# Moving one group of w_in weight sums on VectorE, in a fused linear attention and MLP kernel

## The chip, the cores and the metric

The kernel runs on one core of one Trainium2 chip. The metric is the device time of one execution in microseconds (us), as the median of several runs; lower is better. The engines are named as in the profile: PE is TensorE (matrix products), with PEld for its weight loads, DVE is VectorE, ACT is ScalarE, POOL is GpSimd, and SP is SyncE, which here issues most of the DMAs.

## The reference

The first part is linear attention with a decay per head, worked through in blocks with a running state; the second is a two-layer MLP over its output.

```python
# q, k, v: (4, 8, 768, 64) float32, lam: (8,)
for b in range(nb):                       # blocks of 64 positions
    intra = (qb @ kb^T * Dmask) @ vb      # inside the block, decay lam ** (i - j) for i >= j
    inter = (qb * lam_pow) @ kv_state     # from the state before the block
    out[:, :, sl] = intra + inter
    kv_state = lam_block * kv_state + (kb * rev_pow)^T @ vb
x = out.transpose(0, 2, 1, 3).reshape(3072, 512)
h = x @ w_in                              # (512, 2048)
g = h * sigmoid(1.702 * h)
return g @ w_out                          # (2048, 512)
```

## The kernel before, in words

The 3072 tokens are worked in six waves (0 to 5) of 512 tokens each. A wave goes through the attention part, which leaves its transposed result in `xT`, through the first product with `w_in` and the activation on ACT, which leaves `g_sb`, and through the second product with `w_out`, which goes out to `out`. The waves overlap: while the MLP of wave w runs, the attention of wave w + 1 is made between its steps. Waves 0 and 1 use one layout of the attention (functions with the prefix `d_`, two halves each, called by `start` and `end`), waves 2 to 5 another (prefix `n_`, whose state is carried on from wave to wave).

Both products of the MLP are done, for most of their blocks, in a Strassen-like form with seven products in place of eight. This needs sums and differences of the operands: of the tokens (`x_sums`, line 529, tiles `x_s`; `g_sums`, line 441, tiles `g_s`, whose parts the text calls s1 to s4), and of the weights (`in_sums`, line 520, tiles `w_in_t`; `weight_sums`, line 428, tiles `w_out_t`). All of these are made by DVE. The weight sums are made once and kept. `in_sums(g)` handles group g of the first product's blocks; there are four groups. Groups 0, 1 and 3 are summed in wave 0. Group 2 takes its four blocks from one tile of `w_in`, so its sums are four instructions over 128 x 512 elements, in bf16. Wave 1 uses the sums of groups 0 and 3 alone; waves 2 to 5 use those of all four groups.

The order of the work is written out by hand, with the scheduler set to manual, so each engine's queue has its instructions in the order in which the program calls them. Waves 1 to 5 have a list of steps each in `STEPS`, and `one_step` turns a name into calls. The names that matter here:

- `I2` is `in_sums(2)`.
- `S0` to `S3` are the next wave's scores on PE (line 335). `M0`, `M2` are masks made by DVE alone (line 348), `m1`, `m3` masks scaled by ACT (line 344) and multiplied by DVE (line 345).
- `gl1`, `gl2`, `gh12`, `gl4`, `gh4` are instructions of `g_sums` on DVE.
- `P` with two digits is a product of the second layer on PE (line 461): the first digit is the number of the product, the second the token half. Products 1, 6, 5 and 3 accumulate one behind the other in one PSUM bank, `ps_X`, and what lies in it is read out between them (lines 474 and 485, into `part` and `o_sb`).
- `R` is the rest of the next wave's attention: PE's products (lines 377, 390) and the state products (line 364), which DVE adds to the state in four instructions (line 368).
- `+a1`, `+a2` are the first products of the next wave's first layer (line 544), `X` its `x_sums`, `G` a small copy on POOL that makes it wait for `x_s`. Behind it POOL scales the q and k of the wave after (line 209), and SP transposes them by DMA (line 245).

The steps of wave 1 follow a stretch that isn't in `STEPS`: the end of wave 0's MLP, mixed with the attention of wave 1. There `start(1, 1)` makes scores on PE and masks on DVE (line 267), and `end(1, 0)` and `end(1, 1)` finish with a state update on DVE (line 716).

Of the kernel before, what the change touches and what calls it, by code (L numbers as in the profile page):

```python
# [25 lines left out]
def kernel(  # L26
# [205 lines left out]
    def turn_pe(w, c, nm, copy=act_copy, g=None):  # L232
        x = cast[w, c, nm]
        rr = list(range(NP)) if g is None else [2 * g, 2 * g + 1]
        t = acc("ps_t", bf16, [P, len(rr), 2, P])
        for i, r in enumerate(rr):
            for a in range(2):
                nc.tensor.transpose(t[:, i, a, :], x[:, a, r * P : (r + 1) * P], ident)
        if g in (None, 0):
            trans[w, c, nm] = work.tile([P, 2 * NP, P], bf16, tag=f"{nm}T{c}", bufs={"k": 1, "q": 2}[nm], name=f"{nm}T")  # L240
        copy(trans[w, c, nm][:, 2 * rr[0] : 2 * rr[0] + 2 * len(rr)], t.rearrange("p r a s -> p (r a) s"))
# [323 lines left out]
    def one_step(w, s):  # L565
# [45 lines left out]
        else:  # L611
            raise ValueError(s)

    STEPS = {
# [24 lines left out]
    with tc.manual_schedule():  # L639
# [63 lines left out]
        def end(w, c):  # L703
            oa, oz = d_out(w, c)
            t = acc("ps_kv", shape=[P, NP, D]) if w else states[w, c]
            if w == 0:
                nc.scalar.copy(seen, oz[:, 3, P - 1 : P])
            d_state(w, c, t, Z)
            if w == 0:
                d_inter(w, c, oz, 0, False)  # L710
            if w and c == 0:
                d_one(w, 1)
            d_x(w, c, 0, oa, act_copy)
            d_x(w, c, 1, oz, act_copy if w and c else dve_copy)
            if w:
                nc.vector.tensor_tensor(kv_sb[0][:, 2 * w + c], kept[w, c], t, op=ADD)
            else:
                nc.scalar.copy(kv_sb[0][:, 2 * w + c], t)
            if w and c == 0:
                d_keep(w, 1)  # L720

        def steps(w, names):
            for s in names.split():
                one_step(w, s)
# [21 lines left out]
        steps(0, "P51")  # L746
        turn_pe(1, 1, "k", act_copy)
        end(1, 0)
        steps(0, "P30")
        turn_pe(1, 1, "q", act_copy)  # L750
        halves = [(c, fc) for c in range(HF) for fc in HALVES]
        for i, (c, fc) in enumerate(halves):
# [47 lines left out]
```

## Time and profile before

| | |
|---|---|
| median of 3 runs | 193.56 us (193.47 to 193.85) |
| the profiled execution | 193.77 us, span 192.1 us |
| granted TensorE clock, mean | 1.00 |
| line 520, all 20 instructions on DVE | 20.4 us to 68.5 us after the span's start; the 12 of 128 x 512 take 0.42 us each |

The span runs from the first to the last instruction of the profiled execution; the rest of its time lies around it. The profile gives the start and length of each instruction, the idle time of an engine just before it, and what released it (written `<-`). A line such as `sm<-ps_s` names the tile that is written and the one that is read; `x4` is the count of instructions that are merged into one row. A matmul's end is modelled, so where PE is followed step by step the starts are the better measure.

### The profile page before, as it was taken

Reading aid. Unit: us, or ns where it says so; the run is one execution under the profiler, and the core shown is the slowest. Engines: PE = TensorE matmul, PEld = TensorE weight load, DVE = VectorE, ACT = ScalarE, POOL = GpSimd, SP = SyncE. Lnnn points to the kernel's source line nnn. Section 1 sums busy time; section 2 is a strip of 40 time slices with the busy share of each in tenths; the row PEclk is TensorE's granted clock in tenths of the full one; section 3 lists DMA queues with packets and bytes.
Section 4 is the critical chain, followed back from the end, with each engine's and each line's share of the span. In section 5 each row is a group of like instructions: output and inputs, shape, how many; then the busy total and the mean of one; then the engine's idle time right before and its main releaser. Section 6 shows DMA issues by size and latency. Waiting matters only on the chain.

```text
span 192.1 us, 5543 instructions
## 1 busy us (share of the span) xinstructions
PE 185.1 (96%) x2295; PEld 152.6 (79%) x2297; DVE 153.7 (80%) x292; ACT 129.7 (68%) x242; POOL 53.1 (28%) x76
## 2 busy tenths in 40 slices
PE   7988999999999999999999999999999999999993
PEld 2556645888888887888888888888888888888882
DVE  1777689798477799979799879799889797889950
ACT  4956676257776985379896388895388875597711
POOL 5597000048467000096000295000393000000000
DMA  5999999988997799988998746999365903300113
GB/s 148 322 277 206 206 206 216 275 251 235 238 226 169 172 253 208 221 190 130 209 227 193 237 129 147 216 245 257 109 165 117 212 3 112 110 3 0 52 58 112
DMA packets 89599, 33.91 MB, mean 177 GB/s; under 512 B 67430, under 2 KB 89446, under 8 KB 89574
## 3 DMA queue, kind: packets, MB, share of 16 engines
q1 hardware_dynamic: 84676, 28.84, 60.3%
q0 software_dynamic: 4896, 4.72, 14.3%
q8 instruction: 18, 0.29, 0.7%
q14 instruction: 7, 0.06, 0.1%
q10 hardware_dynamic: 2, 0.00, 0.0%
HBM read 27.26 MB, written 6.29 MB: 175 GB/s over the span
## 4 chain that ended last, share of the span: by engine, by line
PE 80%; DVE 9%; DMA 4%; SPq 3%; issue 1%; ACT 1%; ACTq 0%
PE ps_X L461 20%; PE ps_hX L544 16%; PE ps_V L461 9%; PE ps_hV L544 8%; PE ps_h L402 5%; PE ps_h L414 5%; PE ps_Q L461 5%; PE ps_hQ L544 4%; DMA qf<-in_q_dram 4%; SPq L84 3%; DVE sm L267 2%; DVE g_s L441 2%; PE ps_s L335 2%; PE ps_o L390 2%; DVE sm L348 1%
## 5 line engine op out<-in xcount | busy, mean ns | idle before, releaser
L461 PEld LDWEIGHTS <-g_s 128*128 128x128 bf16 x384 | 36.9, 98 | 5.7 <-DVE g_s L441 0.4
L563 ACT ACTIVATE g_sb<-h_sb 128x512 bf16<-128x512 f32 x54 | 32.6, 631 | 1.2 <-DVE h_sb L552 1.2
L544 PEld LDWEIGHTS <-w_in_t 128*128 128x128 bf16 x288 | 28.2, 98 | 3.3
L461 PEld LDWEIGHTS <-g_sb 128*128 128x128 bf16 x288 | 27.4, 98 | 4.1
L221 ACT COPY part<-ps_hX 128x512 f32<-128x512 f32 x32 | 18.3, 586 | 11.5 <-PE ps_hX L544 11.5
L461 PE MATMUL ps_X<-w_out_t,g_s 128*128 128x256 bf16 x192 | 23.3, 273 | 0.2 <-DVE g_s L441 0.2
L544 PEld LDWEIGHTS <-w_in 128*128 128x128 bf16 x216 | 21.1, 98 | 2.4
L544 PE MATMUL ps_hX<-x_s,w_in_t 128*128 128x256 bf16 x144 | 21.6, 272 | 0.0
L441 DVE TENSOR_TENSOR g_s<-g_sb 128x1024 bf16<-128x1024 bf16 x24 | 16.3, 686 | 6.0 <-ACT g_sb L563 5.6
L209 POOL TENSOR_TENSOR qs<-qf,q_pow 128x512 bf16<-128x512 f32 x16 | 16.7, 1068 | 3.0 <-ACT xT L221 3.0
L209 POOL TENSOR_TENSOR ks<-kf,k_pow 128x512 bf16<-128x512 f32 x16 | 16.6, 1063 | 2.4 <-ACT qT L221 2.4
L634 POOL CAST behind_q<-x_s 1x1 f32<-1x1 bf16 x3 | 0.5, 174 | 59.7 <-DVE x_s L529 59.7
L474 ACT COPY part<-ps_X 128x512 f32<-128x512 f32 (+1 forms) x14 | 7.3, 523 | 13.1 <-PE ps_X L461 13.1
L218 DVE COPY part<-ps_hV 128x512 f32<-128x512 f32 x18 | 12.4, 688 | 4.3 <-PE ps_hV L544 4.3
L552 DVE TENSOR_TENSOR h_sb<-part,ps_hX 128x512 f32<-128x512 f32 x18 | 12.3, 681 | 2.7 <-PE ps_hX L544 2.7
L552 DVE TENSOR_TENSOR h_sb<-part,ps_hV 128x512 f32<-128x512 f32 x18 | 12.3, 683 | 1.0 <-PE ps_hV L544 1.0
L461 PE MATMUL ps_X<-w_out,g_sb 128*128 128x256 bf16 x96 | 12.6, 273 | 0.0
L461 PE MATMUL ps_Q<-w_out,g_sb 128*128 128x256 bf16 x96 | 12.5, 273 | 0.0
L552 DVE TENSOR_TENSOR h_sb<-part,ps_hQ 128x512 f32<-128x512 f32 x18 | 12.2, 679 | 0.0
L221 ACT CAST v_sb<-vf 128x1024 bf16<-128x1024 f32 (+1 forms) x13 | 11.3, 884 | 1.1 <-DMA vf<-in_v_dram 1.0
L461 PE MATMUL ps_V<-w_out_t,g_sb 128*128 128x256 bf16 x96 | 12.0, 273 | 0.0
L461 PE MATMUL ps_X<-w_out,g_s 128*128 128x256 bf16 x96 | 11.6, 272 | 0.2 <-DVE o_sb L485 0.2
(111 smaller groups left out, 358.8 us busy)
## 6 DMA issues: line engine op xcount, KB each, us to landing
kf<-in_k_dram SPq DMA_DIRECT2D x10, 512.0 KB, 6.9
qf<-in_q_dram SPq DMA_DIRECT2D x10, 512.0 KB, 6.7
vf<-in_v_dram SPq DMA_DIRECT2D x10, 512.0 KB, 6.0
out_dram<-o_sb SPq DMA_DIRECT2D x24, 128.0 KB, 2.4
out_dram<-o_sb SPq DMA_DIRECT2D x12, 256.0 KB, 2.9
w_out<-in_moe_w_out_dram POOLq DMA_DIRECT2D x4, 512.0 KB, 15.4
kf<-in_k_dram SPq DMA_DIRECT2D x4, 256.0 KB, 3.1
qf<-in_q_dram SPq DMA_DIRECT2D x4, 256.0 KB, 4.5
```

The lines of the kernel that those rows point to most:

```text
L84: (nc.gpsimd if w == 0 and c and nm == "v" else nc.sync).dma_start(out=x[:, h : h + n], in_=src[2 * w + c, h : h + n, 0 : 2 * P, :].rearra ...
L209: eng.tensor_tensor(x.rearrange("p b (r i j d) -> p j (b r) i d", i=2, j=2, d=D)[:, j], f.rearrange("p h (a d) -> p (h a) d", a=2).rearran ...
L218: nc.vector.tensor_copy(out, in_)
L221: nc.scalar.copy(out, in_)
L402: nc.tensor.matmul(h, w_in_sb[j][:, kc, i * P : (i + 1) * P], xT[w][:, kc, :], start=(kc == 0), stop=(kc == KC - 1))
L414: nc.tensor.matmul(h[:, u, :], w_in_sb[j][:, kc, i * P : (i + 1) * P], xT[w][:, kc, cols], start=(kc == 0), stop=(kc == KC - 1))
L441: nc.vector.tensor_tensor(o, x, y, op=f)
L461: nc.tensor.matmul(bank[:, t], x[:, m, t * P : (t + 1) * P], y, start=(n in (1, 2, 7) and t == ts[0] * last and m == 0), stop=(m == FFC // ...
L474: nc.scalar.copy(part[w, n, t.start][:, t], bank[:, t])
L544: nc.tensor.matmul(bank[:, u], z[:, kc], y[:, kc], start=(n in (1, 2, 7) and u + kc == 0), stop=(kc == 1), skip_group_check=True)
L552: nc.vector.tensor_tensor(h, h_part[w, g, {2: 1, 5: 7, 4: 6}[n]], bank, op=ADD)
L563: nc.scalar.activation(g_of[w][:, a : b + 1 : b - a, 256 * i : 256 * i + 256], bank, GELU)
```

## The change

The step `I2` is taken out of wave 1's list, where it stood between the `g_sums` of `gh3` and the scores and masks of wave 2, and put behind `P30` in the stretch before, right behind `end(1, 0)`. There the DVE instructions in front of it are those of wave 1's first state update (line 716), and the next ones behind it the masks of `start(1, 1)` (line 267). The four instructions and their operands are the same. No other engine gets or loses an instruction, and the order of the others is as before.

```diff
     STEPS = {
-        1: ("a1 a7v a2 a6 b1 b7v A2 a5 b2 b6 B2 a4 a3 b5 b4 A5 P10 A4 b3 gl3 B4 B5 P11 gh3 I2 S0 S1 M0 P20 m1 "
+        1: ("a1 a7v a2 a6 b1 b7v A2 a5 b2 b6 B2 a4 a3 b5 b4 A5 P10 A4 b3 gl3 B4 B5 P11 gh3 S0 S1 M0 P20 m1 "
             "Lk gl1 P70 P71 gl2 P21 v0 gh12 S2 S3 M2 m3 v1 o P40 P41 P60 gl4 gh4 P61 R P50 P51 +a1 X +a2 P30 "
             "P31 "),
...
         end(1, 0)
-        steps(0, "P30")
+        steps(0, "P30 I2")
         turn_pe(1, 1, "q", act_copy)
```

## The prediction

> **What bounds the kernel now.** I began with the busy shares on the page, to see which engine fills the span.
>
> ```profile
> PE 185.1 (96%) x2295; PEld 152.6 (79%) x2297; DVE 153.7 (80%) x292; ACT 129.7 (68%) x242; POOL 53.1 (28%) x76
> ```
>
> TensorE (PE) is busy for 96% of the span, VectorE (DVE) for 80%. So a saving on DVE is worth something only where PE waits for DVE. The next view is the chain of waits, in the stretch around the sums that are moved (line 520); it gives start, length, engine and line.
>
> ```profile
> 66.34 0.69 DVE g_s L441
> 67.03 0.35 DVE w_in_t L520
> 67.38 0.02 issue
> 67.40 0.49 DVE w_in_t L520 x2
> ...
> 79.09 0.61 DVE o_sb L485
> 79.70 0.04 issue
> 79.74 1.91 PE ps_X L461 x16
> ```
>
> From 66.3 to 79.7 us the chain lies on DVE, and the sums are links of it: they are not free where they are. The chain does not say how much a shorter DVE would gain, since PE may have work of its own in that time. Other waves tell that. Waves 1, 2 and 3 issue the same matmuls from the next wave's first scores (line 335, step S0) to step P30 (the last `ps_X<-w_out,g_s` group). I asked for these three stretches. The columns are the stretch, its length, the busy time of PE, PE's weight loads, DVE, ACT and POOL, then the granted clock, the DMA share and GB/s.
>
> ```profile
> 65.96:79.74 13.78, 13.37 (x217) 11.24 (x217) 13.30 (x27) 9.48 (x16) 0.00 (x0) 1.00 1.01 228
> 94.68:107.78 13.10, 13.10 (x218) 11.33 (x218) 11.96 (x23) 9.56 (x17) 0.00 (x0) 1.00 0.99 232
> 122.72:135.81 13.09, 13.09 (x217) 11.31 (x217) 11.95 (x23) 9.55 (x17) 0.00 (x0) 1.00 1.01 244
> ```
>
> The clock was 1.00 in all three and PE's work the same, yet wave 1 takes 13.78 us and the others 13.10 and 13.09. DVE carries four instructions more there (27 against 23): the sums. The excess is 13.78 - 13.10 = 0.68 us. PE's timeline shows where it lies. Wave 1:
>
> ```profile
> 65.96 0.62 PE L335 MATMUL ps_s<-qT,kT 64*128 64x128 bf16 x16
> 72.42 0.60 PE L461 MATMUL ps_X<-w_out_t,g_s 128*128 128x256 bf16 x4
> 73.19 1.48 PE L461 MATMUL ps_X<-w_out_t,g_s 128*128 128x256 bf16 x12 [0.17 <-DVE g_s L441]
> 74.61 0.64 PE L377 MATMUL ps_o<-qT,kv 64*64 64x128 bf16 x32
> 76.70 1.92 PE L461 MATMUL ps_X<-w_out_t,g_s 128*128 128x256 bf16 x16
> 78.46 0.60 PE L544 MATMUL ps_hX<-xT,w_in 128*128 128x256 bf16 x4
> 79.74 1.91 PE L461 MATMUL ps_X<-w_out,g_s 128*128 128x256 bf16 x16 [0.24 <-DVE o_sb L485]
> ```
>
> The same steps in wave 2:
>
> ```profile
> 101.15 1.91 PE L461 MATMUL ps_X<-w_out_t,g_s 128*128 128x256 bf16 x16
> 102.99 0.64 PE L377 MATMUL ps_o<-qT,kv 64*64 64x128 bf16 x32
> 105.08 1.92 PE L461 MATMUL ps_X<-w_out_t,g_s 128*128 128x256 bf16 x16
> 107.78 1.91 PE L461 MATMUL ps_X<-w_out,g_s 128*128 128x256 bf16 x16
> ```
>
> The groups at 72.42 and 101.15 are the steps P60 and P61, those at 76.70 and 105.08 P50 and P51. P60 and P61 take 74.61 - 72.42 = 2.19 us up to the next group in wave 1 and 102.99 - 101.15 = 1.84 in wave 2: in wave 1 PE stops after four matmuls for the upper half of s2 (line 441) and loses 0.35. P30 starts 79.74 - 76.70 = 3.04 after P50 in wave 1 and 107.78 - 105.08 = 2.70 after it in wave 2: it accumulates into the bank that DVE must read first for `o_sb` (line 485), and loses 0.34. Together that is 0.69, the excess of the windows but for rounding.
>
> **What leaves the old place.** DVE's rows there, and one of ACT:
>
> ```profile
> 66.95 0.42 DVE L520 TENSOR_TENSOR w_in_t<-w_in 128x512 bf16<-128x512 bf16 x1
> 68.42 1.40 DVE L348 SCALAR_TENSOR_TENSOR sm<-ps_s,inv_pow,mask 128x512 bf16<-128x512 f32 x2
> 72.45 0.69 DVE L441 TENSOR_TENSOR g_s<-g_s,g_sb 128x1024 bf16<-128x1024 bf16 x1
> 77.44 1.65 DVE L368 SCALAR_TENSOR_TENSOR kv<-kv,blk_pow,ps_kv 128x256 bf16<-128x256 bf16 x4
> 79.01 0.68 DVE L485 TENSOR_TENSOR o_sb<-part,ps_X 128x512 f32<-128x512 f32 x1
> 67.19 1.28 ACT L344 ACTIVATE sm<-ps_s,inv_pow 128x512 bf16<-128x512 f32 x2
> ```
>
> The four sums hold DVE from 66.95 to 68.42, so what is queued behind them can start up to 68.42 - 66.95 = 1.47 us earlier. I follow it step by step. PE's scores of S0 and S1 are done at 65.96 + 0.62 = 66.58, so the masks of line 348 can go at 66.95 and end at 66.95 + 1.40 = 68.35. The next masks want ACT's half of the work, which ends at 67.19 + 1.28 = 68.47: at most 0.12 is lost there. The upper half of s2 then starts at 72.45 - 1.47 = 70.98 and is ready at 71.67, or 0.12 later, before P60 begins at 72.42. The first stall goes whole, with over 0.6 us to spare.
>
> PE is then 0.35 earlier at P50: 76.70 - 0.35 = 76.35. Ahead of it stand the state products that the four updates of line 368 read. DVE could begin the updates at 77.44 - 1.47 = 75.97; waiting for PE it begins at 76.35 at the latest, as the last state product is issued by then, and they end at 76.35 + (79.01 - 77.44) = 77.92. P51 ends 78.46 - 76.70 = 1.76 after P50 begins, at 78.11. So DVE now waits for PE at `o_sb`, not PE for DVE's backlog, as in wave 2, and P30 follows P50 by wave 2's 2.70: 76.35 + 2.70 = 79.05 against 79.74, or 0.69 earlier. What is late next is that same bank, which DVE can read only when P51 is done; waves 2 and 3 have it too.
>
> **What comes into the new place.** DVE's rows there:
>
> ```profile
> 47.22 0.41 DVE L716 TENSOR_TENSOR kv<-half,ps_kv 128x256 bf16<-128x256 f32 x1
> 50.48 2.48 DVE L267 TENSOR_TENSOR sm<-ps_s,mask_d 128x512 bf16<-128x512 f32 x4 [2.85 <-PE ps_s L259]
> ```
>
> Behind the state update (line 716, done at 47.63) DVE idles 2.85 us, until PE's scores release the masks of line 267 at 50.48. At 1.47 us the four sums run from about 47.65 to 49.12 and leave 1.36. The cover is thus DVE's wait for PE. No wait is added that could last: wave 0's dense products have read the same weights by then, and nothing reads the sums before wave 2. Queued behind them on DVE are the masks, then line 716 and `x_s`, and these keep their time as long as the sums end by 50.48. The edit moves no DMA, and PE, ACT, POOL and SP hold the same instructions in the same order in both kernels' listings.
>
> The one neighbour that could lengthen the sums is POOL:
>
> ```profile
> 49.47 2.05 POOL L209 TENSOR_TENSOR ks<-kf,k_pow 128x512 bf16<-128x512 f32 x2 [2.37 <-ACT qT L221]
> 54.47 2.50 POOL L209 TENSOR_TENSOR qs<-qf,q_pow 128x512 bf16<-128x512 f32 x2 [2.95 <-ACT xT L221]
> 56.10 1.15 DVE L529 TENSOR_TENSOR x_s<-x_s,xT 128x512 bf16<-128x512 bf16 x1
> 80.39 0.43 DVE L529 TENSOR_TENSOR x_s<-x_s,xT 128x512 bf16<-128x512 bf16 x1
> ```
>
> One and the same DVE operation, of the sums' shape, took 1.15 us with POOL multiplying beside it and 0.43 with POOL idle. In the new place POOL idles from 49.47 - 2.37 = 47.10 to 49.47, waiting for ACT, so the sums end some 0.3 us before it starts. If the last one slips it costs 0.72 more and still ends about 49.9. I take 1.47 for the four, as in the old place, where POOL was idle too (0.00 in the window); the upper bound is 4 x 1.15 = 4.60. A gain in the new place itself is excluded, as DVE's next work waits for PE either way.
>
> The Trainium skill, "SBUF — State Buffer", section "Who interferes with whom", speaks against the new place, which has POOL's multiplies near: a VectorE instruction with two SBUF inputs contends with a GpSimd instruction that reads SBUF, and whichever comes second is blocked. The two `x_s` rows agree with it (1.15 against 0.43). Were POOL at work throughout, the sum by this rule would be that of the slower rival; with POOL idle it leaves the forecast as it stands.
>
> **Rivals.** Slower: the sums meet POOL's multiplies all along and take 4.60 us, from 47.65 to 52.25. The masks of line 267 start 52.25 - 50.48 = 1.77 late, and PE's products with them by about as much; less the 0.69 won later this is 1.08 slower, 194.64 us. It costs from the point where the four take over 50.48 - 47.65 = 2.83 us, nearly twice their present time, and outweighs the gain at 3.5. For it speaks how close POOL stands, against it that POOL's wait ends with ACT and not with anything moved.
>
> Half the gain: the updates of line 368 get their input later than I take it, `o_sb` with them, and only the first stall goes: 193.56 - 0.35 = 193.21. It bites once they start after 78.11 - 1.57 = 76.54, only 0.19 behind my 76.35, and takes all of the second gain 0.34 later. Against it stands wave 2, which has the same order and no such loss.
>
> Nothing gained: wave 2 can't start its scores earlier, because its transposed q comes no sooner.
>
> ```profile
> 89.59 1.24 SPq L245 DMA_TRANSPOSE qT<-qs  x1
> qT<-qs SPq DMA_TRANSPOSE x8, 2.7
> 94.68 0.62 PE L335 MATMUL ps_s<-qT,kT 64*128 64x128 bf16 x16
> 81.34 0.18 POOL L634 CAST behind_q<-x_s 1x1 f32<-1x1 bf16 x1 [19.97 <-DVE x_s L529]
> ```
>
> The last transpose is issued at 89.59 and lands 2.7 later, at 92.3, which is 2.4 us ahead of the scores at 94.68; the margin is over three times the shift. And the gate at 81.34, which POOL's casts and so the transposes follow, is released by `x_s`, so it moves along. The price would be at most the whole gain: 193.56. The same time would come out if the sums were not where the change says; the listing has them right behind line 716.
>
> **Numbers.** The profiled execution took 193.77 us at a span of 192.1; one like it would take 193.77 - 0.68 = 193.09. It lies 0.21 above the median of the three runs shown (193.56), and that difference I leave as it is: 193.56 - 0.68 = 192.88. A change of 0.2% is 0.39 us, about the least that a measurement of this kernel can tell from none. Chances: the forecast 0.82, half the gain 0.05, nothing gained 0.09 (0.02 of it for sums that are elsewhere), slower 0.04. So faster by over 0.2% has 0.82, within 0.2% 0.05 + 0.09 = 0.14, slower 0.04. The range leaves out the last two cases (0.13): its bottom is the lowest run less the forecast gain, 193.47 - 0.68 = 192.79, its top the case of half the gain, 193.21, each widened by the 0.09 between the lowest run and the median: 192.7 to 193.3.
>
> **What would show it.** Right: rows of line 520 on DVE from about 47.7, of some 0.42 each, and the idle time ahead of line 267 down from 2.85 to about 1.3; the masks of line 348 some 1.5 us earlier, directly behind `g_s`; P60 and P61 in one piece; wave 1's stretch from S0 to P30 at 13.1; later waves the same but 0.68 earlier. Wrong: sums of 1 us with POOL's line 209 beside them, masks of line 267 that start after 50.5, an idle PE ahead of wave 2's scores, or a P60 or P30 that still waits as long.

## The result and the profile after

The changed kernel took 192.63 us (median of 14 runs; 192.19 to 193.53, and one run of 195.44 at a granted clock of 0.982, which the ratio leaves out). The kernel before, run beside it and with its earlier runs, took 193.51 us (14 runs, 192.77 to 194.62). The medians lie 0.88 us apart. The ratio is 0.995, with a 95% interval of 0.9927 to 0.9973: faster by 0.97 us, or anything from 0.52 to 1.41. The profiled execution took 192.84 us at a span of 191.1.

The predicted direction is right, and the predicted 0.68 us lies within that interval. The predicted range does not hold: 192.63 is 0.07 below its bottom of 192.7.

First the stretches of the changed kernel, with the columns as before. The first row is wave 1 from S0 to P30, the second the same in wave 2.

```profile
65.72:78.81 13.09, 13.09 (x217) 11.31 (x217) 12.05 (x23) 9.08 (x16) 0.00 (x0) 1.00 0.97 223
93.74:106.85 13.11, 13.11 (x217) 11.31 (x217) 11.96 (x23) 9.56 (x17) 0.00 (x0) 1.00 1.03 246
46.37:65.72 19.35, 19.18 (x253) 16.61 (x250) 17.02 (x24) 13.96 (x27) 9.07 (x8) 1.00 0.90 209
```

Wave 1 now takes the 13.09 us of the other waves, with 23 instructions on DVE instead of 27. The third row is the part ahead of S0, from the `ps_X<-w_out,g_s` group at 46.37 on, with the new place in it. PE was not busy throughout there, 19.18 of 19.35 us. PE's timeline of the changed kernel shows both:

```profile
46.37 1.05 PE L461 MATMUL ps_X<-w_out,g_s 128*128 128x256 bf16 x8
...
52.77 0.31 PE L316 MATMUL ps_o<-sm,v_sb 64*64 64x128 bf16 x8 [0.17 <-DVE sm L267]
...
72.18 1.91 PE L461 MATMUL ps_X<-w_out_t,g_s 128*128 128x256 bf16 x16
74.02 0.64 PE L377 MATMUL ps_o<-qT,kv 64*64 64x128 bf16 x32
76.11 1.92 PE L461 MATMUL ps_X<-w_out_t,g_s 128*128 128x256 bf16 x16
...
78.81 1.91 PE L461 MATMUL ps_X<-w_out,g_s 128*128 128x256 bf16 x16
```

P60 and P61 run in one piece (74.02 - 72.18 = 1.84), and P30 follows P50 by 78.81 - 76.11 = 2.70: both stalls are gone, at the sizes read off wave 2. But at 52.77 there is a stall: PE waits for a mask of line 267. The kernel before did not have it; there the same 32 matmuls run in one piece:

```profile
52.55 0.77 PE L316 MATMUL ps_o<-sm,v_sb 64*64 64x128 bf16 x32
```

DVE's rows in the new place of the changed kernel, and then POOL's, say why.

```profile
46.74 0.41 DVE L716 TENSOR_TENSOR kv<-half,ps_kv 128x256 bf16<-128x256 f32 x1
47.07 0.42 DVE L520 TENSOR_TENSOR w_in_t<-w_in 128x512 bf16<-128x512 bf16 x1
47.52 0.42 DVE L520 TENSOR_TENSOR w_in_t<-w_in,w_in_t 128x512 bf16<-128x512 bf16 x1
47.87 1.27 DVE L520 TENSOR_TENSOR w_in_t<-w_in 128x512 bf16<-128x512 bf16 x1
49.06 1.26 DVE L520 TENSOR_TENSOR w_in_t<-w_in,w_in_t 128x512 bf16<-128x512 bf16 x1
50.25 2.47 DVE L267 TENSOR_TENSOR sm<-ps_s,mask_d 128x512 bf16<-128x512 f32 x4
```

```profile
47.78 2.27 POOL L209 TENSOR_TENSOR ks<-kf,k_pow 128x512 bf16<-128x512 f32 x2 [1.76 <-DMA kf<-in_k_dram]
```

The first two sums took 0.42 us, the other two 1.27 and 1.26. POOL began to multiply at 47.78, 0.09 ahead of the third. The sums ended at 50.3, the masks no longer waited for PE but for DVE, and the part ahead of S0 grew from 65.96 - 46.85 = 19.11 to 19.35. So the new place was not free in this execution: it cost 0.24.

The whole span, by starts on PE, then reads as follows. The head runs up to the `ps_X<-w_out,g_s` group, the second part from there to S0, the third from S0 to P30, the fourth from P30 to the end, by the span that the trace holds to 0.001 us (192.065 before, 191.141 after). POOL's start is that of its first line 209 row, counted from the end of the head.

| kernel | head | to S0 | S0 to P30 | rest | POOL's start |
|---|---|---|---|---|---|
| before | 46.85 | 19.11 | 13.78 | 112.33 | 2.62 |
| changed | 46.37 | 19.35 | 13.09 | 112.33 | 1.41 |

The span is 0.92 us shorter: 0.48 in the head, where nothing is edited, and 0.69 from S0 to P30, less 0.24 in the second part; the rest is the same to 0.01. The experiments ask which of these the change makes.

### The profile page after: what moved, and what is told of

Its sections match the earlier page's. It is cut to its first block, busy times and chain, and to the rows that moved or that the text cites. A ratio compares the mean times of both kernels' runs of the same rounds, so it can differ in the third digit from the quotient of the medians.

```text
span 191.1 us, 5544 instructions
## 1 busy us (share of the span) xinstructions
PE 184.6 (97%) x2297; PEld 152.2 (80%) x2297; DVE 156.3 (82%) x292; ACT 129.6 (68%) x242; POOL 53.7 (28%) x76
## 4 chain that ended last, share of the span: by engine, by line
PE 73%; DMA 11%; DVE 8%; POOL 2%; ACT 2%; issue 1%; SPq 0%; ACTq 0%
PE ps_X L461 19%; PE ps_hX L544 16%; PE ps_V L461 9%; PE ps_hV L544 8%; PE ps_Q L461 5%; DMA w_in<-in_moe_w_in_dram 5%; PE ps_hQ L544 4%; DVE w_in_t L520 3%; DMA kf<-in_k_dram 3%; DMA vf<-in_v_dram 3%; PE ps_h L414 2%; PE ps_s L335 2%; PE ps_o L390 2%; PE ps_fill L147 2%; POOL ks L202 1%; DVE sm L267 1%
## 5 line engine op out<-in xcount | busy, mean ns | idle before, releaser
L563 ACT ACTIVATE g_sb<-ps_hX 128x512 bf16<-128x512 f32 x18 | 10.6, 588 | 1.8 <-PE ps_hX L544 1.8
L461 PE MATMUL ps_V<-w_out_t,g_s 128*128 128x256 bf16 x96 | 11.6, 273 | 0.0
```

Of the source, the lines that this page charges most:

```text
L461: nc.tensor.matmul(bank[:, t], x[:, m, t * P : (t + 1) * P], y, start=(n in (1, 2, 7) and t == ts[0] * last and m == 0), stop=(m == FFC // ...
L563: nc.scalar.activation(g_of[w][:, a : b + 1 : b - a, 256 * i : 256 * i + 256], bank, GELU)
```

## The experiments

The first theory is that the change gives 0.69 and pays 0.24 when POOL begins before the third sum, and that the head is chance. The rivals are that the head belongs to the change, and that the 0.24 belongs to the place and not to POOL. The four parts of all profiled executions come first; each kernel is then taken up, with its edit against the changed kernel.

| kernel | head | to S0 | S0 to P30 | rest | POOL's start |
|---|---|---|---|---|---|
| changed, again | 46.41 | 19.35 | 13.09 | 112.33 | 1.31 |
| changed, POOL behind the fourth sum | 46.33 | 19.11 | 13.09 | 112.35 | 2.52 |
| sums behind the second state update | 47.17 | 21.27 | 13.10 | 112.35 | 1.74 |
| sums in wave 0 | 46.45 | 19.12 | 13.09 | 112.33 | 1.72 |
| before, again | 47.33 | 19.12 | 13.79 | 112.34 | 1.69 |
| one sum moved | 48.11 | 19.12 | 13.33 | 112.34 | 1.75 |
| two sums moved | 46.88 | 19.11 | 13.10 | 112.34 | 2.06 |
| no sums | 47.22 | 19.11 | 13.10 | 112.32 | 2.57 |
| changed, POOL behind the first sum | 45.82 | 19.11 | 13.10 | 112.34 | 1.91 |
| changed, POOL behind the second sum | 45.93 | 19.11 | 13.09 | 112.35 | 2.14 |
| changed, third profile | 47.46 | 19.12 | 13.09 | 112.35 | 2.40 |
| changed, fourth profile | 47.08 | 19.11 | 13.10 | 112.34 | 1.91 |

**The changed kernel again.** No edit.

> The changed kernel once more, unedited, for a second profile beside the kernel before. I split the execution at three starts on PE: the head, up to the `ps_X<-w_out,g_s` group in front of the new place's transposes (46.85 us before, 46.37 after); from there to S0 (19.11 before, 19.35 after); from S0 to P30 (13.78 before, 13.09 after); and the rest. Theory: the two stalls (0.69) are gone for good, the head's 0.48 is chance, since nothing is edited there, and the 0.24 that the second part lost comes from POOL's first line 209 instruction starting at 47.78 while the sums ran, so it is there again only if POOL starts before about 48.6. Expected: S0 to P30 13.1; second part 19.1 to 19.4 according to POOL's start; head anywhere from 46.3 to 47.0. Rival: the change shortens the head too (by something that I don't see); then the head is near 46.4 again and the whole is 0.9 faster. Time by the theory 0.45 to 0.7 us under the kernel before, by the rival 0.9.

192.55 us against 193.26 (33 runs), ratio 0.9948 (0.9925 to 0.997). POOL began at 1.31, and the second part was 19.35 again. The head of 46.41 and the 1.0 us that the ratio gives (0.58 to 1.45) are what the rival expected, so it stands for now.

**POOL held back.**

```diff
         steps(0, "P30 I2")
+        gate_pool(TI[2][3][0:1, 0, 0, 0:1])
```

> The changed kernel with one small POOL copy that reads the last of the four sums, put right behind them, so that POOL's multiplies (line 209) can't start while the sums run. Theory (POOL's multiplies lengthened the last two sums from 0.42 to 1.27 and 1.26 us and so held up the masks of line 267): all four sums take 0.42, the masks start with PE's scores again, the second part is 19.1 and S0 to P30 13.1; POOL's multiplies start 1 to 2 us later than they could, and nothing waits for them, since their q comes later still. Time 0.7 us under the kernel before. Rival (the sums are long for another reason, DMA traffic or the place itself): two of them still take 1.2 us and more and the second part stays at 19.35.

`gate_pool` is the small copy on POOL of one element (line 634); POOL's queue reaches its multiplies only behind it.

The rows of DVE and then of POOL in this kernel:

```profile
47.03 0.42 DVE L520 TENSOR_TENSOR w_in_t<-w_in 128x512 bf16<-128x512 bf16 x1
47.48 0.43 DVE L520 TENSOR_TENSOR w_in_t<-w_in,w_in_t 128x512 bf16<-128x512 bf16 x1
47.83 0.42 DVE L520 TENSOR_TENSOR w_in_t<-w_in 128x512 bf16<-128x512 bf16 x1
48.16 0.42 DVE L520 TENSOR_TENSOR w_in_t<-w_in,w_in_t 128x512 bf16<-128x512 bf16 x1
49.96 2.48 DVE L267 TENSOR_TENSOR sm<-ps_s,mask_d 128x512 bf16<-128x512 f32 x4 [1.38 <-PE ps_s L259]
```

```profile
48.71 0.18 POOL L634 CAST behind_q<-w_in_t 1x1 f32<-1x1 bf16 x1 [2.22 <-DVE w_in_t L520]
48.85 2.04 POOL L209 TENSOR_TENSOR ks<-kf,k_pow 128x512 bf16<-128x512 f32 x2
```

The same four instructions in the same place take 0.42 each, DVE has 1.38 us left before the masks, which wait for PE again, and the second part is 19.11. So the place is not at fault. The time was 192.51 us, ratio 0.995 (0.9925 to 0.9975); next to the changed kernel's 0.9948, the 0.24 is too small to be seen in the times.

**The sums beside POOL.**

```diff
-        steps(0, "P30 I2")
+        steps(0, "P30")
...
                 end(1, 1)
+                steps(0, "I2")
```

> The four sums behind the second state update of wave 1 (line 716, at 53.6 us) instead of the first, right ahead of `x_s`, where POOL's multiplies run from 53.0 to 59.8 us. Theory (POOL's multiplies lengthen sums): the four take 1.15 to 1.27 each, 4.6 to 5 us in all, `x_s` starts near 59 and not at 54.2, and PE waits for it ahead of the first `ps_hV<-x_s` group: the second part is 1.3 to 2.0 us longer than 19.1, S0 to P30 13.1; time 0.6 to 1.3 us over the kernel before. Rival (place and POOL don't matter, four sums are 1.47 us): `x_s` starts 1.5 us later and is ready in time, the second part stays at 19.1, time 0.7 under the kernel before.

DVE, POOL, and the two places where PE waited, in this kernel:

```profile
54.46 0.88 DVE L520 TENSOR_TENSOR w_in_t<-w_in 128x512 bf16<-128x512 bf16 x1
55.37 1.15 DVE L520 TENSOR_TENSOR w_in_t<-w_in,w_in_t 128x512 bf16<-128x512 bf16 x1
56.44 1.26 DVE L520 TENSOR_TENSOR w_in_t<-w_in 128x512 bf16<-128x512 bf16 x1
57.63 1.26 DVE L520 TENSOR_TENSOR w_in_t<-w_in,w_in_t 128x512 bf16<-128x512 bf16 x1
58.82 2.45 DVE L529 TENSOR_TENSOR x_s<-xT 128x512 bf16<-128x512 bf16 x2
```

```profile
54.01 2.23 POOL L209 TENSOR_TENSOR qs<-qf,q_pow 128x512 bf16<-128x512 f32 x2 [3.05 <-DMA qf<-in_q_dram]
56.20 2.41 POOL L209 TENSOR_TENSOR ks<-kf,k_pow 128x512 bf16<-128x512 f32 x2
58.58 2.41 POOL L209 TENSOR_TENSOR qs<-qf,q_pow 128x512 bf16<-128x512 f32 x2
```

```profile
60.14 0.60 PE L544 MATMUL ps_hV<-x_s,w_in_t 128*128 128x256 bf16 x4 [1.22 <-DVE x_s L529]
61.79 0.61 PE L544 MATMUL ps_hX<-x_s,w_in_t 128*128 128x256 bf16 x4 [0.62 <-DVE x_s L529]
```

With POOL multiplying all along, the four sums hold DVE from 54.46 to 58.82, 4.36 us where the old place took 1.47. `x_s` is late and PE stands twice; the second part is 21.27, or 2.16 longer (expected 1.3 to 2.0; the second stall had not been counted). The time was 195.25 us, ratio 1.0083 (1.0049 to 1.0117), that is 1.6 us slower, where 0.6 to 1.3 was expected; the parts give 2.16 - 0.69 = 1.47. This is the slower rival of the prediction, one state update later.

**The sums in wave 0.**

```diff
-        steps(0, "P30 I2")
+        steps(0, "P30")
...
-            steps(0, {5: "I1", 7: "I3", 9: "I0 gl3 gl1", 11: "W01234 gl2", 13: "W11234 gl4"}.get(fc, ""))
+            steps(0, {5: "I1", 7: "I2 I3", 9: "I0 gl3 gl1", 11: "W01234 gl2", 13: "W11234 gl4"}.get(fc, ""))
```

> The four sums in wave 0, ahead of group 3's sums, where DVE waited 1.2 us (before) and 1.6 us (after) for a DMA of w_in, and POOL has no arithmetic. Theory: 0.42 each, 1.5 in all, mostly inside that wait; group 3's sums and what follows may be up to 0.5 us later and DVE makes that up before PE needs its second-layer sums; so head as in the kernel before (46.3 to 47.0), second part 19.1, S0 to P30 13.1, time 0.7 us under the kernel before, the best of these four with the gated one. Rival (DVE is short of time in wave 0, too): PE waits in the head for `g_s` or `w_out_t`, head about 1 us longer, time the same as the kernel before or slower.

The parts are those of the kernel with POOL held back: 19.12 and 13.09, with a head of 46.45. 192.51 us, ratio 0.994 (0.9913 to 0.9967). The sums fit into DVE's wait for w_in, of which 1.09 us is left behind them, and POOL has no arithmetic near them.

**The kernel before as its own change.** No edit.

> The kernel before, unedited, as if it were a change. It gives a second profile of the kernel before, with its head. Theory (the head, up to the `ps_X<-w_out,g_s` group, varies by chance, as nothing ahead of it is edited in the changed kernel; it was 46.85 us before and 46.33 to 47.17 in the five edited ones): ratio 1.000 within its interval; a head anywhere from 46.3 to 47.2; second part 19.11, S0 to P30 13.78. Rival (the changes shorten the head): a head of 46.85 again, as in the first profile.

193.4 us against 193.6 (23 runs), ratio 0.9986 (0.996 to 1.0013). The second and third part repeated to 0.01 us, the head did not: 47.33 after 46.85. The two profiles of the kernel before differ in the head alone.

**One sum and two sums moved.** `in_sums` gets a list of the sums to make; in the first kernel the first is made in the new place and the other three in the old, in the second kernel two and two.

```diff
-    def in_sums(g):
+    def in_sums(g, which=(0, 1, 2, 3)):
...
-            for o, x, y in ((t1, b12, b11), (t2, b22, t1), (t3, b22, b12), (t4, b21, t2)):
+            ops = ((t1, b12, b11), (t2, b22, t1), (t3, b22, b12), (t4, b21, t2))
+            for o, x, y in [ops[n] for n in which]:
```

> Only the first of the four sums moved to the new place, the other three left ahead of wave 2's masks. It tells how the two stalls depend on DVE's backlog. By the rows of before it takes 67.40 - 66.95 = 0.45 us out of the old place: the upper half of s2 is ready at 73.14 - 0.45 = 72.69, ahead of PE's want at 72.86, so the first stall goes whole; P30 still waits for `o_sb`, which ends 0.45 earlier. Theory (P30 is set by DVE's backlog until that is gone): S0 to P30 is 13.78 - 0.45 = 13.33. Rival (the two stalls are paid off in proportion to what is moved, a quarter of 0.69): 13.61.

> The first two of the four sums moved, two left. They hold DVE from 66.95 to 67.74, 0.79 us, which is more than the 0.69 that the stalls cost. Theory: S0 to P30 is 13.09 to 13.1 already, as with all four moved, and the other two could stay for nothing; the two moved end some 0.8 us behind the state update, before POOL's line 209 begins, so the second part is 19.11. Rival (in proportion): 13.78 - 0.35 = 13.43.

PE's timeline of the kernel with one sum moved:

```profile
67.23 0.62 PE L335 MATMUL ps_s<-qT,kT 64*128 64x128 bf16 x16
73.69 1.91 PE L461 MATMUL ps_X<-w_out_t,g_s 128*128 128x256 bf16 x16
77.62 1.92 PE L461 MATMUL ps_X<-w_out_t,g_s 128*128 128x256 bf16 x16
80.56 1.91 PE L461 MATMUL ps_X<-w_out,g_s 128*128 128x256 bf16 x16
```

S0 to P30 is 80.56 - 67.23 = 13.33, as the theory said: P60 and P61 in one piece, P30 still 80.56 - 77.62 = 2.94 behind P50. With two moved it is 13.10, all of the gain. So PE pays for DVE's backlog only beyond a point, and half of the sums could have stayed. Each of these two kernels ran once, in 194.7 and 193.13 us; the first is the longer by its head of 48.11, so the times say nothing here.

**No sums.** Group 2's products read group 1's sums, so this kernel leaves out a part of the product; it bounds what any place for the sums can give.

```diff
     TI = {g: [...] for g in USED}
+    TI[2] = TI[1]
...
-        steps(0, "P30 I2")
+        steps(0, "P30")
```

> The four sums left out, with group 2's products reading group 1's sums in their place, so that part of the product is not computed as it should be. It bounds what any place for the sums can give. Theory: second part 19.11, S0 to P30 13.09, time 0.69 us under the kernel before, no more than with the sums moved and POOL held back. Rival (the sums cost something else, in the head or later, which the moved ones still pay or which the move frees): a part other than S0 to P30 is shorter than in the kernel before, and the time is 0.9 or more under it.

192.8 us against 193.6, ratio 0.9954 (0.9921 to 0.9988); 19.11 and 13.10, and a head of 47.22. Against the kernel before only the part from S0 to P30 is shorter, by 0.68: nothing but the two stalls is to be had from the sums.

**From which start of POOL it costs.** The gate of the second experiment, reading the first (`TI[2][0]`) or the second sum (`TI[2][1]`) instead of the fourth.

> The changed kernel with POOL's small copy reading the first of the four sums, so that POOL's multiplies start about 0.3 us behind the end of that sum, or later if k has not landed. It tells from which point POOL's start costs time. With the `ps_X<-w_out,g_s` group as zero, the sums begin at 0.70, 1.15, 1.50 and 1.83, and the masks of line 267 can go at about 3.6. Theory (each sum that begins while POOL multiplies takes 1.27 and not 0.42, and only what ends behind 3.6 costs): POOL starts at about 1.4, the third and fourth sums take 1.27 each and end at 3.9, second part 19.3 to 19.35. Rival (the cost does not depend on POOL's start but on the place): 19.35 whenever POOL starts.

> As the kernel with the copy behind the first sum, but with the copy reading the second sum. Theory: POOL starts at about 1.85, only the fourth sum takes up to 1.27, it ends at about 3.1 to 3.2, before the masks can go, and the second part is 19.11 as with no meeting at all. Rival (any meeting costs, in proportion): about 0.12 more, 19.23.

Neither made the case that it was meant for: k landed later than the gate opened, so POOL began at 1.91 and 2.14, that is 0.07 and 0.31 us behind the start of the fourth sum, with that sum alone beside it. All sums took 0.42 and the second part was 19.11 (one execution each, 192.07 and 192.18 us). The rival that the place costs 0.24 at any start of POOL falls with them; the dose is not measured.

**The changed kernel, two more profiles.** No edit.

> The changed kernel, unedited, for another profile. In the first two POOL's line 209 began 1.41 and 1.31 us behind the `ps_X<-w_out,g_s` group, ahead of the third sum (1.50), and the second part was 19.35 both times; in the kernels where the sums were elsewhere or POOL was free it began at 1.69 to 2.62. The open question is how often the changed kernel pays the 0.24. Theory (chance in when k's load is issued; a sum is lengthened only if it begins behind POOL's first instruction): second part 19.35 if POOL begins ahead of 1.50, 19.11 if later, and a look like this can have either. Rival (the place itself): 19.35 at any start of POOL.

> The same as the look before, once more: second part 19.35 if POOL's line 209 begins less than 1.50 us behind the `ps_X<-w_out,g_s` group, 19.11 if it begins later; S0 to P30 13.1, the part behind P30 112.3. Rival (the place itself): 19.35 at any start of POOL.

POOL began at 2.40 and 1.91, and the second part was 19.12 and 19.11 with sums of 0.42. DVE and POOL in the last one:

```profile
48.58 0.42 DVE L520 TENSOR_TENSOR w_in_t<-w_in 128x512 bf16<-128x512 bf16 x1
48.92 0.42 DVE L520 TENSOR_TENSOR w_in_t<-w_in,w_in_t 128x512 bf16<-128x512 bf16 x1
```

```profile
48.99 2.26 POOL L209 TENSOR_TENSOR ks<-kf,k_pow 128x512 bf16<-128x512 f32 x2 [1.75 <-DMA kf<-in_k_dram]
```

Here POOL began 0.07 us behind the fourth sum, which kept its 0.42. So the unedited changed kernel paid 0.24 in two of four executions, those in which POOL began before the third sum, and nothing in the other two. Its head ran from 46.37 to 47.46. These last two executions took 193.81 and 193.42 us, more than the 192.77 of the kernel before beside them: a single execution shows the head, not the change.

## Why the prediction was right or wrong

**The two stalls: right.** 0.35 and 0.34, 0.69 in all, were forecast from wave 2's steps, and S0 to P30 is 13.09 or 13.10 in all nine profiles in which the four sums had left the old place, and in the one without sums. P30 follows P50 by the 2.70 forecast. DVE's rows of the changed kernel show the order that the prediction gave: the upper half of s2, the updates of line 368, and `o_sb`.

```profile
70.74 0.69 DVE L441 TENSOR_TENSOR g_s<-g_s,g_sb 128x1024 bf16<-128x1024 bf16 x1
...
75.97 1.66 DVE L368 SCALAR_TENSOR_TENSOR kv<-kv,blk_pow,ps_kv 128x256 bf16<-128x256 bf16 x4 [0.15 <-PE ps_kv L364]
78.07 0.69 DVE L485 TENSOR_TENSOR o_sb<-part,ps_X 128x512 f32<-128x512 f32 x1 [0.44 <-PE ps_X L461]
```

The upper half of s2 starts 5.02 us behind S0, as forecast (70.98 - 65.96), and is ready before P60 at 72.18; the updates and `o_sb` now wait for PE. The rest kept its length (112.32 to 112.35 in all profiles), so nothing was given back there. Half the gain and nothing gained are out, as rivals.

**The new place: the step that failed in the mechanism.** The prediction had POOL idle until 49.47 because it waits for ACT's copy of qT, and concluded that its start would stay clear of the sums. That was read from the releaser in POOL's row. In the profile after, the same row names the load of k. Here is the issue of that load by SP, in the kernel before and then in the changed one, with ACT's copy in the changed one:

```profile
44.09 3.24 SPq L88 DMA_DIRECT2D kf<-in_k_dram  x2
```

```profile
42.46 3.21 SPq L88 DMA_DIRECT2D kf<-in_k_dram  x2
...
47.90 1.01 ACT L221 COPY qT<-ps_t 128x1024 bf16<-128x1024 bf16 x1 [0.28 <-PE ps_t L238]
```

ACT's copy began at 47.90, behind POOL's start at 47.78, so POOL can't have waited for it. From the issue of the load to POOL's start it was 49.47 - 44.09 = 5.38 us before and 47.78 - 42.46 = 5.32 after, and in both traces the first of the load's two DMAs lands 5.2 us behind its issue: it was the load both times. So the margin of 0.3 us rested on a transfer, whose start against PE changes from one execution to the next (POOL's start lies between 1.31 and 2.62 in the tables, leaving out the three gated kernels). The price that the prediction gave to a sum beside POOL, 1.15, was nearly right (1.27); that the last sum alone could slip was not: two did. The threshold of the slower rival, 2.83 us for the four, was passed: they took 3.18, from 47.07 to the masks at 50.25, which by that threshold would cost 0.35. But the prediction gave a chance to no meeting and to one all along, and to none between, so the cost of 0.24 was none of its cases.

The rule of the Trainium skill that was weighed there ("SBUF — State Buffer", section "Who interferes with whom") speaks of an instruction that comes second being blocked, and the traces bear that out in its order: the sum that began 0.09 behind POOL took 1.27, the one that began 0.07 ahead of it 0.42. By that rule alone the place would have been judged by who begins first, which is the question that decided.

**The number and the range: too narrow.** The forecast difference was 0.68. The parts give 0.69 or 0.45, and the times 0.97 (0.52 to 1.41; 0.88 between the medians), 1.0 at the repetition (0.9948; 0.58 to 1.45). The step that failed is the last one of "Numbers": it widened the range by 0.09 us, the distance between the lowest and the middle of three runs that happened to lie within 193.47 to 193.85, as if two medians could differ from the truth by no more. The runs showed that they can. The kernel before, unedited, has medians of 193.51, of 193.26 on one chip, and of 193.4 and 193.6 in two sets on another, 0.34 apart, and single runs from 192.57 up. A bottom widened by 0.34 would have been at 192.45.

If the other parts keep their lengths in all runs as they do in the profiles, what the medians have beyond them lies in the head, which ran from 45.82 to 48.11 over the fourteen profiles and which only the kernel with the sums in wave 0 edits. An estimate of the heads of all runs, each run's span less the other three parts, gives means of 46.6 us for the kernel before (66 runs), 46.3 with POOL held back (11), 46.6 without sums (12), and 46.1 to 46.4 for the changed kernel (25), the less the more often it paid 0.24; within one kernel they scatter by 0.3 to 0.7. So a steady shortening of the head by the change is not shown, and one of 0.2 is not excluded. What makes the head vary was not followed up and stays open. So does the mean gain: the parts give 0.45 when POOL comes early and 0.69 when not, without telling how often, and the two intervals hold 0.69 and just leave out 0.45.

**The best version.** With the sums in wave 0, or POOL held back, the meeting can't occur: 32.21 and 32.20 us from the head to P30, against 32.44 for the changed kernel when it pays (32.21 when it does not) and 32.89 before. In the times they can't be told from the changed kernel (0.994 and 0.995 against 0.995 and 0.9948).

## What to carry to other kernels

To price work on a side engine, compare a wave that has it with waves that don't, start by start on the bottleneck engine: 1.47 us of DVE was worth 0.69, in two stalls, and half of the work could have stayed for nothing. When you move work into an engine's idle time, ask not only who is idle beside it but what ends that idleness, and when that is a transfer, take its start as loose by a microsecond and more. A releaser named in one profile is a guess where several were awaited; a second profile, or the time at which the load landed, shows the true one.

## What the runs showed of the hardware

A DVE sum of two operands in SBUF (128 x 512, bf16) that began while POOL multiplied took longer than the 0.42 us that it takes alone: 1.27 and 1.26 in the changed kernel, 0.88 to 1.26 with the sums beside POOL. The masks of line 267, which read one operand from PSUM, did not: four took 2.48 us in the kernel before, where POOL worked from 49.47 to 51.52 beside the first of them, and 2.47 in the changed one, where POOL was done by 50.05. And the order of the starts decided who paid, by less than 0.1 us: where the sum began 0.07 us first, in the fourth profile of the changed kernel and with POOL behind the first sum, it kept its 0.42, and POOL's first multiply took 1.25 and 1.26 us instead of the 1.04 with POOL behind the fourth sum, its pair 2.26 instead of 2.04.
